# Gated linear attention and a top-1 mixture of experts in one kernel: the fullest expert's first layer is given 320 places early, at the end of the attention part's plan

## The chip, the cores and the metric

The kernel runs on one core of a Trainium2 chip. The core has a matrix engine (TensorE, PE in the rows below), a vector engine (VectorE, DVE), a scalar engine for activations (ScalarE, ACT), a general engine (GpSimd, POOL) and a queue engine (SyncE, SP), each with its own stream of instructions. SP, ACT and POOL also trigger DMA transfers. SBUF is the working memory; PE writes to the eight banks of PSUM. The metric is device time in microseconds (us); the profile comes from one further execution with the hardware profiler.

## What the reference computes

```python
# attention: 4 sequences, 8 heads, 768 steps, 48 features; a complex state per head
a = (a_re + i a_im), scaled so that |a| <= 0.999
S_t = a_t * S_(t-1) + k_t v_t^T          # a_t scales the rows of S
y_t = q_t . Re(S_t)
# the y of all heads side by side are the tokens of the second part
x = y reshaped to (3072, 384)
logits = x @ w_gate                      # 8 experts
e = argmax(logits); g = softmax(logits)[e]
out = g * (relu(x @ w1[e]) @ w2[e])      # w1: 384 x 1024, w2: 1024 x 384, each expert its own
```

## The kernel before

**Attention.** The time axis is cut into units of 128 to 384 steps (`UNITS`, ten of them) and chunks of 128 (24 in all, six for each sequence b = 0 to 3). `front(u)` turns gates, q and k of a unit into scaled operands: logarithms, exponentials and sines on ACT, scans and products on DVE and some on POOL. Its last products go to the tile `zp`, and DMAs on SP move `zp` into `hz0` or `hz1`, the operand buffers that PE reads. `chunk(b, c)` works on PE: scores (L416, masked by DVE into `am`), transposed keys (L409), the products with the state (L428) and with v (L435), the new state (L443), and a product with `turn` (L451) whose result, the tokens with their logits, ACT copies to `xg` (L454).

**Routing.** `route(b, r0, r1)` takes some chunks' tokens: DVE finds the largest logit (L467 and following, `lg` to `oh`), PE counts places (L492 to L497), DVE makes the row numbers `slot` (L504), and POOL scatters the tokens, a chunk at a time, into `xs_hbm` in device memory (L511), which has 480 places for each expert. The last sequence is routed in three pieces: chunks 0 to 2, 3 and 4, and 5. After its chunk 2, `ranks()` sorts the experts by their count so far into `order` (L533).

**Experts.** The experts go in `TURNS`, the fullest first. `weights(e)` loads w1 and w2 (1.5 MB each); `tokens(e)` loads the expert's places from `xs_hbm` into `xb` with four DMAs (for e = 0 two of them from ACT) and DVE transposes them into `xrt` (L686). `expert(e)` makes the first layer in eight groups of three matmuls, each group into a bank of its own (L701), with a relu to `ht` by ACT (L707) or DVE (L704) in turns; then the second layer in tiles of 128 places (L720), scaled by DVE (L651) and scattered by POOL (L640). An fp32 matmul is two records in the trace, so an expert's first layer is 48 records.

**What sets the order.** Each part is a `Plan`: every step names its engine, an estimated duration and the keys that it reads and writes, and `order()` searches with some randomness for a good order. The engines then run their streams as emitted, with waits for data and for buffers. Attention (P) and experts (M) are two plans. The matmuls, tiles and memory of the two parts are apart, and M is planned with `routed` 27 us after its start:

```python
        M.add("", 27.0, lambda: None, (), ("routed",))
        M.add("PE", 22.0, lambda: None, (), ("turned",))
```

Of the kernel before, what the change touches and what calls it, by code (L numbers as in the profile page):

```python
# [37 lines left out]
XR = 9  # L38
MINC = 256
# [128 lines left out]
def gateloop_then_moe(ctx, tc, gates, qk, v, wg, w1, w2, out):  # L168
# [68 lines left out]

    with ExitStack() as att:
# [4 lines left out]
        bAB, bZ = buf("AB", 2, [128, 2, G, TU]), buf("Z", 2, [128, 2, G, TU])  # L243
# [4 lines left out]
        zp, = buf("zp", 1, [128, 2, 2 * G * TU])  # L248
# [6 lines left out]
        hz = buf("hz", 2, [128, 2 * H * TU])  # L255
# [38 lines left out]
        def front(u):  # L294
# [50 lines left out]
            for g in range(G):  # L345
                P.add("DVE", 2 * T * 0.00105 + 0.19, lambda g=g: nc.vector.tensor_tensor_scan(
                    si[:, g, :], ones_t[:, sl], im[:, g, :], tend[:, b, g, c0:c0 + 1], ALU.mult, ALU.add),
                    (Bk, ("tend", b, c0)), (("si", g),))
# [107 lines left out]
        def route(b, r0, r1):  # L456
# [52 lines left out]
            for c in range(n):  # L509
# [6 lines left out]
                P.add("POOL", 1.27, f, (slot, ("xg", (g0 + c) % XR), ("empty", 0), ("empty", 1), ("empty", 2)), (("rows", b, r0 + c),), lat=2.0, wire=0.6)  # L516

        def ranks():
# [16 lines left out]
            P.add("", 14.0, lambda: None, ("order",), ("prefetch",))  # L535
# [44 lines left out]


    again = consts.tile([1, 1], I32, name="again")
    ok = consts.tile([128, 4], FP32, name="ok")
    f1 = consts.tile([128, NU], FP32, name="f1")
    nc.vector.tensor_scalar(out=f1, in0=chk, scalar1=5.0625, scalar2=None, op0=ALU.is_le)
    nc.vector.tensor_reduce(ok[:, 0:1], f1, axis=AX, op=ALU.min)
    lv = lend.rearrange("p b g c -> p (b g) c")
    f2 = consts.tile([128, B * G, C], FP32, name="f2")
    tt(f2, lv[:, :, 1:], lv[:, :, :C], ALU.subtract)
    nc.vector.tensor_scalar(out=f2, in0=f2, scalar1=-60.0, scalar2=None, op0=ALU.is_ge)  # L590
    nc.vector.tensor_reduce(ok[:, 1:2], f2.rearrange("p a c -> p (a c)"), axis=AX, op=ALU.min)
    f3 = consts.tile([128, B * G], FP32, name="f3")
    nc.vector.tensor_scalar(out=f3, in0=lv[:, :, C], scalar1=-100.0, scalar2=None, op0=ALU.is_ge)
    nc.vector.tensor_reduce(ok[:, 2:3], f3, axis=AX, op=ALU.min)
    nc.tensor.matmul(bank[7][:, 0:E], lhsT=ones_b, rhs=cumb, start=True, stop=True)
    f4 = consts.tile([128, E], FP32, name="f4")
    tt(f4, bank[7][:, 0:E], base, ALU.subtract)
    f5 = consts.tile([128, E], FP32, name="f5")
    nc.vector.tensor_scalar(out=f5, in0=f4, scalar1=float(MINC), scalar2=None, op0=ALU.is_ge)
    caps = consts.tile([128, E], FP32, name="caps")  # L600
    for x in range(E):
        nc.gpsimd.memset(caps[:, x:x + 1], float(CAPS[x]))
    tt(tmp, pick, bc(f4[:, None, :], [128, E, E]), ALU.mult)
    nc.vector.tensor_reduce(f4, tmp, axis=AX, op=ALU.add)
    tt(f4, f4, caps, ALU.is_le)
    tt(f4, f4, f5, ALU.mult)
    nc.vector.tensor_reduce(ok[:, 3:4], f4, axis=AX, op=ALU.min)
    okm = consts.tile([128, 1], FP32, name="okm")
    nc.vector.tensor_reduce(okm, ok, axis=AX, op=ALU.min)
    nc.tensor.matmul(bank[7][0:1, 64:65], lhsT=okm, rhs=one, start=True, stop=True)  # L610
    nc.vector.tensor_scalar(out=again, in0=bank[7][0:1, 64:65], scalar1=127.5, scalar2=None, op0=ALU.is_lt)


    with ExitStack() as ms:
# [17 lines left out]
        ev = xs_hbm.rearrange("(e s) w -> e s w", e=E)
        ENG = (mybir.EngineType.SP, mybir.EngineType.Activation)
        which = {}
# [20 lines left out]
        def weights(e):  # L655

            def f():
                which[e] = ds(nc.values_load(order[0:1, TURNS[e]:TURNS[e] + 1], engines=ENG[0:2 if e == 0 else 1], min_val=0, max_val=E - 1,
                                             skip_runtime_bounds_check_because="experts have numbers below E"), 1)
# [30 lines left out]
        def expert(e):  # L690
            s, n, h = e % 2, CAPS[TURNS[e]], e % NH
            if e:
                weights(e)
# [198 lines left out]
```

## Time and profile before

| | us |
|---|---|
| median of 3 runs (lowest, highest) | 545.51 (544.99, 546.72) |
| the profiled execution | 545.12 |
| its span, first to last instruction | 543.4 |
| PE busy | 455.4 (84%) |
| DVE busy | 269.5 (50%) |
| ACT busy | 201.2 (37%) |
| POOL busy | 113.7 (21%) |

The page cuts the span in 40 slices of 13.6 us and gives the busy share of each in tenths. PE is near 9 in slices 9 to 17 (attention), 3 and 4 in slices 18 and 19, and 9 or more from there on (experts). DVE is at 9 through most of slices 1 to 13 and at 1 among the experts. PE's busy time includes matmuls that run at half clock, and a matmul's end is modelled, so gaps between groups of records say more than the share.

### The profile page before, as it was taken

The page shows a single profiled execution, that of the slowest core. Times are in us where ns is not written, and L with a number is a line of the kernel's source. Part 1 is how long each engine was busy: PE and PEld are TensorE (multiplying, and loading weights), DVE is VectorE, ACT ScalarE, POOL GpSimd, SP SyncE. Part 2 cuts the span into 40 slices and gives each one's busy share as a digit, 9 for nine tenths or more (in the row PEclk, how much of TensorE's full clock was granted, in tenths as well). Part 3 has the DMA queues.
Part 4 walks back from the last instruction along what each step waited for, and adds up shares of the span by engine and source line. Part 5 has one row for each costly group of instructions (what it writes and reads, how often), then busy time and mean ns, then how long its engine had stood idle before and what let it go on. Part 6 is the DMA issues. An engine that isn't in the chain of part 4 may idle for free. (4 is left out here: it accounts for less than half of the span.)

```text
span 543.4 us, 7115 instructions
## 1 busy us (share of the span) xinstructions
PE 455.4 (84%) x2690; PEld 320.0 (59%) x2690; DVE 269.5 (50%) x432; ACT 201.2 (37%) x289; POOL 113.7 (21%) x125
## 2 busy tenths in 40 slices
PE   0046879298988989993499999999999999999995
PEld 0035769297877979992245554555555555555553
DVE  6989999999999799743121211002111111111111
ACT  6968888977787756641000100000000000000000
POOL 6263042173302450252000010210200011012102
PEclk9997669688989989997599999999999999999998
DMA  8596493969999775265992770141823370001001
GB/s 262 162 259 190 135 265 115 281 168 316 258 254 260 190 225 154 58 213 216 284 326 55 268 200 1 36 145 36 283 84 91 117 261 15 16 19 43 29 3 54
DMA packets 47226, 86.19 MB, mean 159 GB/s; under 512 B 21057, under 2 KB 36700, under 8 KB 45137
## 3 DMA queue, kind: packets, MB, share of 16 engines
q1 hardware_dynamic: 42704, 75.20, 47.9%
q0 software_dynamic: 3200, 9.86, 4.9%
q10 hardware_dynamic: 1280, 0.61, 0.5%
q8 instruction: 23, 0.38, 0.3%
q14 instruction: 19, 0.15, 0.1%
HBM read 53.93 MB, written 13.24 MB: 124 GB/s over the span
## 5 line engine op out<-in xcount | busy, mean ns | idle before, releaser
L701 PE MATMUL bank<-xrt,w1b 128*128 128x416 f32 (+3 forms) x384 | 141.1, 521 | 10.9 <-DVE xrt L686 10.9
L720 PE MATMUL bank<-w2b,ht 128*128 128x384 f32 (+1 forms) x512 | 138.7, 487 | 0.0
L701 PEld LDWEIGHTS bank<-xrt,w1b 128*128 128x128 f32 x384 | 73.8, 193 | 72.9 <-issue 39.9
L720 PEld LDWEIGHTS bank<-w2b,ht 128*128 128x128 f32 (+1 forms) x512 | 76.7, 170 | 59.0 <-issue 11.6
L707 ACT ACTIVATE ht<-bank 128x416 f32<-128x416 f32 (+3 forms) x32 | 16.5, 517 | 255.9 <-PE bank L701 255.9
L416 PE MATMUL bank<-hz 128*128 128x128 f32 x384 | 63.7, 324 | 38.8 <-DMA hz<-zp 38.4
L416 PEld LDWEIGHTS bank<-hz 128*128 128x128 f32 x384 | 58.0, 234 | 41.2 <-issue 39.1
L640 POOL DMA_INDIRECT out_dram<-yo,gi x24 | 23.6, 982 | 255.2 <-DVE yo L651 238.4
L704 DVE TENSOR_SCALAR ht<-bank 128x416 f32<-128x416 f32 (+3 forms) x32 | 18.9, 590 | 114.0 <-PE bank L701 110.3
L651 DVE TENSOR_SCALAR yo<-bank,gi 128x384 f32<-128x384 f32 x24 | 14.8, 618 | 92.7 <-PE bank L720 92.7
L181 DVE TENSOR_TENSOR zp<-Z,cs 128x1152 f32<-128x1152 f32 (+2 forms) x40 | 48.4, 1246 | 0.5 <-DMA hz<-zp 0.2
L435 PE MATMUL bank<-am,v 128*48 128x128 f32 x384 | 28.7, 290 | 11.6 <-DVE am L181 11.4
L181 DVE TENSOR_TENSOR am<-bank,causal 128x512 f32<-128x512 f32 x48 | 32.2, 681 | 11.4 <-PE bank L416 7.8
L181 POOL TENSOR_TENSOR AB<-AB,C 128x1152 f32<-128x1152 f32 (+2 forms) x9 | 20.8, 2316 | 75.7 <-ACT C L280 68.1
L511 POOL DMA_INDIRECT xs_hbm<-xg,slot x24 | 27.7, 1154 | 41.2 <-DVE slot L504 23.2
L443 PE MATMUL bank<-v,kt 128*96 128x48 f32 x320 | 33.8, 263 | 2.6 <-ACT kt L411 2.6
L443 PEld LDWEIGHTS bank<-v,kt 128*96 128x96 f32 x320 | 32.5, 181 | 3.6 <-ACT kt L411 2.7
L451 PE MATMUL bank<-turn,yt 128*128 128x104 f32 x192 | 30.5, 309 | 2.9 <-ACT yt L439 1.8
L181 POOL TENSOR_TENSOR Z<-Z,AB 128x1152 f32<-128x1152 f32 (+2 forms) x9 | 22.2, 2470 | 48.1 <-ACT AB L280 42.6
L335 DVE TENSOR_TENSOR_SCAN D<-AB,lend,C 128x384 f32<-128x384 f32 (+2 forms) x30 | 31.1, 1074 | 0.3
L578 ACT ACT_TABLE_LOAD x23 | 29.5, 1283 | 3.3 <-DVE cs L351 2.2
L451 PEld LDWEIGHTS bank<-turn,yt 128*128 128x128 f32 x192 | 27.1, 218 | 5.9 <-ACT yt L439 2.7
(122 smaller groups left out, 434.4 us busy)
## 6 DMA issues: line engine op xcount, KB each, us to landing
w1b<-in_w_dram SPq DMA_DIRECT2D x8, 1536.0 KB, 6.7
w2b<-in_w_dram SPq DMA_DIRECT2D x8, 1536.0 KB, 10.2
hz<-zp SPq DMA_DIRECT2D x24, 432.0 KB, 7.5
AB<-in_gates_dram SPq DMA_DIRECT2D x12, 576.0 KB, 4.8
Z<-in_qk_dram SPq DMA_DIRECT2D x12, 576.0 KB, 5.0
v<-in_v_dram SPq DMA_DIRECT2D x8, 576.0 KB, 8.0
hz<-zp SPq DMA_DIRECT2D x8, 288.0 KB, 4.5
hz<-zp SPq DMA_DIRECT2D x12, 192.0 KB, 7.1
```

The lines of the kernel that those rows point to most:

```text
L181: (eng or nc.vector).tensor_tensor(out=o, in0=a, in1=b, op=op)
L335: P.add("DVE", 2 * T * 0.00105 + 0.19, lambda g=g: nc.vector.tensor_tensor_scan(d[:, g, :], a[:, g, :], c[:, g, :], lend[:, b, g, c0:c0 + ...
L416: nc.tensor.matmul(SC[hf][:, (h % 4) * 128:(h % 4) * 128 + 128], lhsT=hk[:, h], rhs=hq[:, h], start=True, stop=True)
L435: nc.tensor.matmul(YT[ps, (h // 2) * 128:(h // 2) * 128 + 128], lhsT=V[:, cl, h * D:h * D + D], rhs=am[2 * par + hf][:, h % 4, :], start=( ...
L443: nc.tensor.matmul(ST[0:96, h * D:h * D + D], lhsT=kt[par][:, h * 96:h * 96 + 96], rhs=V[:, cl, h * D:h * D + D], start=(c == 0 and h == 0 ...
L451: nc.tensor.matmul(XT[:, p * 104:p * 104 + 104], lhsT=yt[par][:, p * 128:p * 128 + 128], rhs=turn[:, p, :], start=True, stop=True)
L511: i = nc.gpsimd.indirect_dma_start(out=xs_hbm[:, :], out_offset=bass.IndirectOffsetOnAxis(ap=R[slot][:, c:c + 1], axis=0), in_=xg[:, (g0 + ...
L578: nc.scalar.preload_act_table_set("natural_log_exp_and_others" if P.cur == "LE" else "trig_and_small")
L640: i = nc.gpsimd.indirect_dma_start(out=out[:, :], out_offset=bass.IndirectOffsetOnAxis(ap=index, axis=0), in_=y, in_offset=None, bounds_ch ...
L701: nc.tensor.matmul(HB[hb][:, 0:n], lhsT=w1b[e % NW][:, c:c + 128], rhs=xrt[s][:, d, 0:n], start=(d == 0), stop=(d == DT - 1))
L704: M.add("DVE", 0.6, lambda f_=f_, hb=hb: nc.vector.tensor_scalar_max(ht[h][:, f_, 0:n], HB[hb][:, 0:n], 0.0), (("H", hb),), (("ht", h, f_),))
L720: nc.tensor.matmul(OB[ob][p0:p0 + m, 0:DM], lhsT=ht[t % NH][:, f_, c0:c0 + m], rhs=w2b[t % NV][:, f_ * DM:f_ * DM + DM], start=(f_ == 0), ...
```

## The change

The first 320 places of the fullest expert (`EARLY` = 10 blocks of 32) are loaded, transposed and put through the first layer at the end of the attention plan. They hold only tokens that were routed by chunk 2 of the last sequence. The other 160 places follow in the expert plan as before, into the same `ht`. The buffers `hz`, `AB`, `Z` and `zp` of attention serve as the first two pairs of weight buffers, as `xb`, as `xrt` and as the first `ht`. The scatter of a chunk that is added to the attention plan after the early rows waits until those are loaded (the keys `xbA`). The check of the kernel's own assumptions moves into the expert plan, and `front` of the last unit is added to the plan ahead of the chunks of the unit before it.

```diff
+EARLY = 10
+    w1b, w2b = [z[:, 0:DT * F] for z in hz], [z[:, DT * F:2 * DT * F] for z in hz]
+    xb = [... for t in bAB]
+    xrt = [... for t in bZ]
+    ht = [zp...]
...
 -                P.add("POOL", 1.27, f, (slot, ..., ("empty", 2)), (("rows", b, r0 + c),), lat=2.0, wire=0.6)
+                P.add("POOL", 1.27, f, (slot, ..., ("empty", 2)) + tuple(("xbA", x) for x in range(4)), (("rows", b, r0 + c),), lat=2.0, wire=0.6)
...
+        def early_rows():
+...
+            P.add("SP", 0.5, lambda: which.update({0: expert_of(0, mybir.EngineType.SP)}), ("order",), (("which", 0),))
+            for i in range(4):
+                last = P.add("SP", 0.65, lambda i=i: nc.sync.dma_start(
+                    xb[0][32 * i:32 * i + 32, None, 0:EARLY, :], xv[:, which[0], 0:EARLY, 104 * i:104 * i + 96]),
+                    (("which", 0), "xb0") + tuple(("rows", B - 1, c) for c in range(3)), (("xbA", i),), lat=2.0, wire=0.8)
+            for z in range(2):
+                P.add("SP", 0.65, f, (("which", 0), "hz0"), (("w1", 0, z),), lat=1.9, wire=2.6)
+            P.add("SP", 0.65, lambda: nc.sync.dma_start(w2b[0][:, None, :], w2v[:, which[0], :]), ..., after=[last])
+            for j in range(0, EARLY, 4):
+                P.add("DVE", ..., lambda j=j, j1=j1: turn_rows(0, j, j1), ..., (("xrtA", j),))
+
+        def early_layer():
+            n = 32 * EARLY
+            for f_ in range(FT):
+                bk, key = ((bank[7], "ones"), (bank[3], ("KT", 1)), (bank[5], "ST"))[f_ % 3]
+                def f(f_=f_, bk=bk):
+                    for d in range(DT):
+                        c = d * F + f_ * 128
+                        nc.tensor.matmul(bk[:, 0:n], lhsT=w1b[0][:, c:c + 128], rhs=xrt[0][:, d, 0:n], start=(d == 0), stop=(d == DT - 1))
+                P.add("PE", 1.5, f, (("w1", 0, f_ // 4),) + tuple(("xrtA", j) for j in range(0, EARLY, 4)), (key,))
+                P.add("ACT", act_t(n), lambda f_=f_, bk=bk: nc.scalar.activation(ht[0][:, f_, 0:n], bk[:, 0:n], func=ACT.Relu),
+                      (key, "ht0"), (("htA", f_),))
...
-                front(u)
+                if u < NU - 1:
+                    front(u)
+                if u == NU - 2:
+                    front(NU - 1)
+                    early_rows()
...
+            early_layer()
             for i in P.order():
...
-        M.add("", 27.0, lambda: None, (), ("routed",))
-        M.add("PE", 22.0, lambda: None, (), ("turned",))
+        M.add("", 6.0, lambda: None, (), ("routed",))
...
-            s, nb = e % 2, CAPS[TURNS[e]] // 32
+            s, n0, nb = e % 2, 0 if e else EARLY, CAPS[TURNS[e]] // 32
...
-                        nc.tensor.matmul(HB[hb][:, 0:n], lhsT=w1b[e % NW][:, c:c + 128], rhs=xrt[s][:, d, 0:n], ...)
+                        nc.tensor.matmul(HB[hb][:, 0:n - n0], lhsT=w1b[e % NW][:, c:c + 128], rhs=xrt[s][:, d, n0:n], ...)
```

The order of instructions around the seam follows. PE, from the last product of attention on; before, what comes next is the count for the last chunk's route, the check and then the first expert's layer:

```order
L451 MATMUL bank6_67<-turn_97,yt1_155 128x104 x4
L492 LDWEIGHTS before_108
L492 MATMUL bank2_63<-oh_168,before_108 128x8
L494 LDWEIGHTS ones_b_111
L494 MATMUL bank2_63<-cumb_125,ones_b_111 128x8
L595 LDWEIGHTS ones_b_111
L595 MATMUL bank7_68<-cumb_125,ones_b_111 128x8
L610 MATMUL bank7_68<-one_73,okm_2033 1x1
L701 MATMUL bank0_61<-xrt0_2047,w1b0_2040 128x480 x3
L701 MATMUL bank1_62<-xrt0_2047,w1b0_2040 128x480 x3
```

In the changed kernel the same place reads as follows; the line numbers are those of the changed kernel (L473 is the product with `turn`, L514 and L516 are the count, L590 the early layer), `hz0` holds w1 and `Z0` the transposed tokens:

```order
L473 MATMUL bank6_67<-turn_97,yt1_160 128x104 x4
L590 MATMUL bank7_68<-Z0_137,hz0_139 128x320 x3
L514 LDWEIGHTS before_108
L514 MATMUL bank2_63<-oh_171,before_108 128x8
L516 LDWEIGHTS ones_b_111
L516 MATMUL bank2_63<-cumb_125,ones_b_111 128x8
L590 MATMUL bank5_66<-Z0_137,hz0_139 128x320 x3
L590 MATMUL bank7_68<-Z0_137,hz0_139 128x320 x3
L590 MATMUL bank3_64<-Z0_137,hz0_139 128x320 x3
```

One group of the early layer now stands ahead of the last chunk's count and seven behind it (the other four in banks 7, 3, 5 and 3). After these come the first two tiles of the expert's second layer, 16 matmuls of 128x384, then the eight groups of 128x160 for its other places.

ACT, from the copy of the last chunk's tokens on, before; L670 are its two triggers of loads of the first expert's rows:

```order
L454 COPY xg0_158<-bank6_67 128x416
L477 ACTIVATE ex_164<-sub_163 128x8
L658 TENSOR_LOAD order_123
L670 ISA
L670 DMA xb0_2062<-xs_hbm 32x15x96
L670 ISA
L670 DMA xb0_2062<-xs_hbm 32x15x96
L707 ACTIVATE ht0_2049<-bank0_61 128x480
```

And ACT in the changed kernel; L592 is the relu of the early layer, L736 the load of the expert's last five blocks of rows:

```order
L476 COPY xg0_163<-bank6_67 128x416
L499 ACTIVATE ex_167<-sub_166 128x8
L592 ACTIVATE zp_141<-bank7_68 128x320
L592 ACTIVATE zp_141<-bank5_66 128x320
L256 TENSOR_LOAD order_123
L736 ISA
L736 DMA AB0_135<-xs_hbm 32x5x96
L592 ACTIVATE zp_141<-bank7_68 128x320
L736 ISA
L736 DMA AB0_135<-xs_hbm 32x5x96
L592 ACTIVATE zp_141<-bank3_64 128x320
```

Two relus of the early layer stand ahead of the first trigger, one between the two triggers, and five behind.

DVE, at the route of the last chunk, in the changed kernel; L260 transposes the early rows:

```order
L489 TENSOR_REDUCE lg_128<-xg0_163 128x8
L489 TENSOR_REDUCE mx_165<-lg_128 128x1
L260 STREAM_TRANSPOSE Z0_137<-AB0_135 128x4x3x32 x2
L260 STREAM_TRANSPOSE Z0_137<-AB0_135 128x2x3x32
L182 TENSOR_TENSOR sub_166<-lg_128,mx_165 128x8
L506 SCALAR_TENSOR_TENSOR eq_169<-sub_166,rev_106 128x8
```

Before, `sub` followed `mx` at once; now the three transposes of the early rows stand between them, behind the two steps that read the last chunk's logits.

## Rows read from the trace of the kernel before

**Rows 1.** PE's waits from 262 us on: us in total, times, longest.

```profile
PE bank L701 <- DVE xrt L686: 10.9, 1, 10.9
```

**Rows 2.** Windows: us, busy by engine (records), then PE clock, DMA share, GB/s.

```profile
200.00:225.00 25.00, 25.00 (x248) 24.07 (x246) 23.66 (x57) 17.42 (x30) 3.30 (x3) 0.88 0.46 125
...
260.00:543.00 283.00, 272.09 (x896) 150.52 (x896) 47.53 (x87) 16.54 (x32) 25.53 (x26) 0.98 0.37 112
```

**Rows 3.** Timeline around the seam: start, us, work, count [idle before and its releaser].

```profile
247.30 0.98 POOL L511 DMA_INDIRECT xs_hbm<-xg,slot  x1 [0.31 <-issue]
...
247.80 1.14 PE L451 MATMUL bank<-turn,yt 128*128 128x104 f32 x8 [0.74 <-ACT yt L439]
...
249.51 0.21 DVE L467 TENSOR_REDUCE lg<-xg 128x8 f32<-128x32 f32 x1 [3.44 <-ACT xg L454]
...
252.54 0.16 DVE L504 TENSOR_REDUCE slot<-z 128x1 int32<-128x8 f32 x1 [1.03 <-DMA xs_hbm<-xg,slot]
...
253.58 0.99 POOL L511 DMA_INDIRECT xs_hbm<-xg,slot  x1 [5.09 <-DVE tmp L181]
...
257.44 2.23 SPq L670 DMA_DIRECT2D xb<-xs_hbm  x4
257.51 1.20 ACTq L670 DMA_DIRECT2D xb<-xs_hbm  x2
...
263.72 0.35 SPq L662 DMA_DIRECT2D w1b<-in_w_dram  x1
263.78 1.85 DVE L686 STREAM_TRANSPOSE xrt<-xb 128x384 f32<-128x384 f32 x4 [8.78 <-DMA xb<-xs_hbm]
...
265.70 19.75 PE L701 MATMUL bank<-xrt,w1b 128*128 128x480 f32 x42 [10.87 <-DVE xrt L686]
```

**Rows 4.** Timeline of the step that makes the early rows possible, columns as in Rows 3.

```profile
239.07 0.22 DVE L533 TENSOR_REDUCE order<-tmp 128x8 int32<-128x64 f32 x1
239.19 0.98 POOL L511 DMA_INDIRECT xs_hbm<-xg,slot  x1 [0.30 <-issue]
...
240.33 0.38 SPq L662 DMA_DIRECT2D w1b<-in_w_dram  x1
```

**Rows 5.** The tile xb from 230 to 300 us: landing of its loads.

```profile
DMA to landing us min/median/max: 3.0/4.8/15.5
```

**Rows 6.** Timeline: weight loads and matmuls at full clock, columns as in Rows 3.

```profile
271.60 0.19 PEld L701 LDWEIGHTS bank<-xrt,w1b 128*128 128x128 f32 x1 [0.21 <-issue]
...
272.00 0.19 PEld L701 LDWEIGHTS bank<-xrt,w1b 128*128 128x128 f32 x1 [0.21 <-issue]
...
285.29 2.74 PE L720 MATMUL bank<-w2b,ht 128*128 128x384 f32 x8
```

**Rows 7.** Timeline of earlier PE work: two waits, and a group of scores.

```profile
129.36 0.65 PE L435 MATMUL bank<-am,v 128*48 128x128 f32 x8 [2.07 <-DVE am L181]
...
154.71 0.98 PE L435 MATMUL bank<-am,v 128*48 128x128 f32 x8 [1.92 <-DVE am L181]
...
241.73 1.08 PE L416 MATMUL bank<-hz 128*128 128x128 f32 x8
```

**Rows 8.** Windows of 1 us after waits of PE, columns as in Rows 2.

```profile
131.00:132.00 1.00, 1.00 (x9) 1.00 (x8) 1.00 (x2) 1.00 (x2) 0.00 (x0) 0.50 1.00 336
137.00:138.00 1.00, 1.00 (x7) 0.95 (x5) 0.58 (x1) 1.00 (x2) 0.00 (x0) 0.59 1.04 283
154.00:155.00 1.00, 0.29 (x4) 0.29 (x6) 1.00 (x3) 1.00 (x2) 0.00 (x0) 0.94 0.87 171
158.00:159.00 1.00, 0.55 (x8) 0.25 (x4) 1.00 (x1) 0.59 (x2) 0.00 (x0) 0.86 1.08 221
...
270.00:271.00 1.00, 1.00 (x3) 0.53 (x2) 0.00 (x0) 0.04 (x1) 0.00 (x0) 0.54 1.13 479
```

**Rows 9.** Groups by shape, ACT from 250 us on: busy us, mean ns, idle before.

```profile
L707 ACT ACTIVATE ht<-bank 128x384 f32<-128x384 f32 x12 | 5.9, 490 | 93.1 <-PE bank L701 93.1
```

More of the change, by code (lines that the diff above doesn't have):

```diff
@@ L236, in gateloop_then_moe, with expert_of, turn_rows @@
     nc.gpsimd.memset(empty.bitcast(I32)[:, W - 1:W], 1 << 20)
+    keep = ctx.enter_context(tc.tile_pool(name="keep", bufs=1))
+    bAB, bZ, hz = ([keep.tile(shp, FP32, name=f"{nm}{i}") for i in range(2)] for nm, shp in (
+        ("AB", [128, 2, G, TU]), ("Z", [128, 2, G, TU]), ("hz", [128, 2 * H * TU])))
+    zp = keep.tile([128, 2, 2 * G * TU], FP32, name="zp")
+    w1b, w2b = [z[:, 0:DT * F] for z in hz], [z[:, DT * F:2 * DT * F] for z in hz]
+    xb = [t.rearrange("p a g t -> p (a g t)")[:, 0:CAP * 3].rearrange("p (n c) -> p n c", c=96) for t in bAB]
+    xrt = [t.rearrange("p a g t -> p (a g t)")[:, 0:CAP * DT].rearrange("p (d c) -> p d c", d=DT) for t in bZ]
+    ht = [zp.rearrange("p a t -> p (a t)")[:, 0:FT * CAP].rearrange("p (f c) -> p f c", f=FT)]
+    w1v, w2v = (w.rearrange("(e p) f -> p e f", p=128) for w in (w1, w2))
+    xv = xs_hbm.rearrange("(e j p) w -> p e j w", e=E, p=32)
+    sv = xs_hbm.rearrange("(e s) w -> s e w", e=E)
+    ev = xs_hbm.rearrange("(e s) w -> e s w", e=E)
+    which = {}
+    def expert_of(e, eng):
+        return ds(nc.values_load(order[0:1, TURNS[e]:TURNS[e] + 1], engines=(eng,), min_val=0, max_val=E - 1,
+                                 skip_runtime_bounds_check_because="experts have numbers below E"), 1)
+    def turn_rows(s, b0, b1):
+        nc.vector.transpose(xrt[s][:, :, 32 * b0:32 * b1].rearrange("p d (b t) -> p b d t", t=32),
+                            xb[s][:, b0:b1].rearrange("p b (d c) -> p b d c", d=DT))
     with ExitStack() as att:
@@ L515, in f @@
                     tc.add_to_no_dep_group("rows", i.ins)
-                P.add("POOL", 1.27, f, (slot, ("xg", (g0 + c) % XR), ("empty", 0), ("empty", 1), ("empty", 2)), (("rows", b, r0 + c),), lat=2.0, wire=0.6)
+                P.add("POOL", 1.27, f, (slot, ("xg", (g0 + c) % XR), ("empty", 0), ("empty", 1), ("empty", 2)) + tuple(("xbA", x) for x in range(4)), (("rows", b, r0 + c),), lat=2.0, wire=0.6)
         def ranks():
@@ new lines, in early_layer @@
+        def early_layer():
[9 more added lines that the diff above has]
+                      (key, "ht0"), (("htA", f_),))
+            P.add("seam", 7.0, lambda: None, tuple(("rows", B - 1, c) for c in range(C)), ("seam",))
@@ L591, in gateloop_then_moe @@
[L591 to L608, printed above, removed]
@@ L655, in weights @@
         def weights(e):
-            def f():
-                which[e] = ds(nc.values_load(order[0:1, TURNS[e]:TURNS[e] + 1], engines=ENG[0:2 if e == 0 else 1], min_val=0, max_val=E - 1,
-                                             skip_runtime_bounds_check_because="experts have numbers below E"), 1)
-            M.add("SP", 0.3, f, (), (("which", e),), after=rows[-1:])
+            M.add("SP", 0.5, lambda: which.update({e: expert_of(e, mybir.EngineType.SP)}), (), (("which", e),), after=rows[-1:])
             for wb, wv, nb, nm in ((w1b, w1v, NW, "w1"), (w2b, w2v, NV, "w2")):
@@ L728, in gateloop_then_moe @@
         with tc.manual_schedule():
-            weights(0)
             for e in range(E):
                 expert(e)
+                if e == 0:
+                    check(M)
                 if e < E - 1:
@@ L735, in gateloop_then_moe @@
                     M.add("PE", 0.5, lambda: flag.append(nc.values_load(again[0:1, 0:1], min_val=0, max_val=1, skip_runtime_bounds_check_because="0 or 1")),
[L736 removed]
+                          (("H", 0), "again"), ())
             for i in M.order():
```

110 lines of the change are left out of this document (69 added, 41 removed).

## The prediction

> **What bounds the kernel now.** I read the slices of the page first, then the waits of PE, then the seam between attention and experts instruction by instruction, and last the order of both kernels there. From 262 us on PE has one single wait, for the transposed tokens of the first expert [rows 1], and in 260 to 543 us it is busy for 272.09 of 283 us at a clock of 0.98 [rows 2]. So the expert part is bound by PE alone: what PE starts earlier at the seam comes off the end one for one, as long as no later wait takes its place. At the seam PE ends the last product of attention at 247.80 + 1.14 = 248.94 us, which I call E, and starts the first expert's layer at 265.70 [rows 3]. Between stand 16.76 us in which PE has three tiny counts to do.
>
> What fills them is a chain without slack: the logits of the last chunk reach DVE at 249.51; the row numbers at 252.54 wait 1.03 us until the scatter of chunk 4, started at 247.30, has landed (5.2 us); the last scatter starts at 253.58 and has landed at 257.44 (3.9 us), when SP and ACT trigger the loads of the rows; the transposes start at 263.78 and PE at 265.70 [rows 3]. The pause has a second price: PE comes back at half clock. The first 42 records took 19.75 us [rows 3], while at full clock one starts every 0.40 us [rows 6], 16.8 us in all; the difference is 2.9 us, and the clock rose in the slice of 270 us [rows 8].
>
> **The change part by part.** All is reckoned from E. At full clock the work of PE from the first expert matmul to the end is 543.40 - 265.70 - 2.9 = 274.8 us.
>
> *The early layer itself.* 48 records of 320 columns, at 0.40 us for 480 columns [rows 6] 0.267 us each, are 12.8 us. The 48 records of 160 columns are 6.4 us by their columns; a group of eight records with 128 columns takes 1.08 us, 0.135 each [rows 7], and a weight load 0.19 [rows 6], so 6.4 to 9.1 us; I take 0.145 each, 7.0, near the 128-column row. Together 19.8 in place of 19.2. With 0.2 for the counts of the check, which used to lie in the pause, 274.8 - 19.2 + 7.0 + 0.2 = 262.8 us are left behind the early layer.
>
> *When it can start.* The ranks were known at 239.29, w1 was triggered at 240.33, and the third scatter of the last sequence started at 239.19 [rows 4]. With 3.9 to 5.2 us to land, four triggers of some 0.6 us (four took 2.23 [rows 3]) and 3.0 to 4.8 us for the loads [rows 5], the early rows would be there between 248.3 and 251.4. In the new order PE has some 2.5 us more of attention's work left behind the count for the ranks than before, so I take L, their landing, as E. On DVE the transposes now stand behind the first two steps of the last chunk's route, which end about E + 1.0. Four transposes of 15 blocks took 1.85 us [rows 3]; three of 10 blocks take 1.3 to 1.5. PE starts at **E + 2.5**. A gap of that size brings half clock: after waits of 2.07 and 1.92 us [rows 7] the clock went down within two us and stayed down from about 131.0 to 137.8 and from 154.9 to 158.3 [rows 8], which costs 1.7 to 3.4 us of PE work.
>
> *Where it stops.* Each group is 1.6 us and needs a free bank. Four groups run without a further relu than the first two. The fifth goes to bank 7 again and needs the third relu, and on ACT a trigger for the last rows stands ahead of that relu. That trigger waits for the last scatter. SP shows that a waiting trigger holds what is behind it: the second expert's w1, which waits for no rows, was triggered only at 263.72, behind the row loads [rows 3]. I take ACT to do the same; the other end is that it holds nothing. The trigger is set free so: the scatter of chunk 3 now waits for L, that of chunk 4 starts 1.3 later and lands 5.2 later, at E + 6.8; slot and scatter as before 1.04 later, landing 3.9 later, **E + 11.7** (before: E + 8.5). Then 0.6 for the trigger (two took 1.20 [rows 3]), 0.45 for a relu of 320 (0.49 for 384 [rows 9]) and 0.2 for two hand-overs: the fifth group starts at E + 12.9. The first four, 6.4 us and 3.4 for the clock from E + 2.5 on, with the count of 0.2 between, end by E + 12.5, so the clock's price is hidden under the hold. Four groups more: the early layer ends at **E + 19.3**.
>
> The Trainium skill says the same of ACT: TensorE: Matmul & The Clock Gate, Part 1, on the engines' queues, has the scalar engine work strictly first in, first out. By that rule the hold is sure and the time is the forecast; were it not so, the time would be that of the first rival. No run here yet shows ACT behind a waiting trigger.
>
> *What I cost at nothing.* The last five blocks of rows: triggered by E + 13.2, landed 4.8 later [rows 5], transposed by E + 19; PE has 32 records of the second layer first, at 2.74 us for eight [rows 6] 11 us, so they are needed at E + 30 and have 11 us of cover. The second expert's w1 goes behind the row loads as before, at about 265 against 263.72, and is needed at E + 39: cover of more than 10 us. The check's steps on DVE lie beside experts' matmuls, where DVE is busy for 47.53 of 283 us [rows 2]. If a cover fails, its excess falls on PE in full.
>
> *Attention.* The instructions up to the seam are the same, but the order is searched anew. In 200 to 225 us DVE is busy for 23.66 of 25 us and PE all the time, at a clock of 0.88 [rows 2]: a new order has little idle time to win on DVE; it can dodge that dip (12% of 25, 3.0 us) or meet one more like that of 131 us (3.4 us). I take 0, with -4 to +4.
>
> *Sum.* With E = 248.94 the span ends at 248.94 + 19.3 + 262.8 = 531.0, 12.4 us under 543.4. The profiled execution took 545.12, 0.4 below the median of the runs, so 532.7 to 533.1: **533 us**.
>
> **Rivals.** *Nothing holds ACT*, or the last scatter lands by the time the relu is due. Then the layer runs through, E + 2.5 + 12.8 + 0.2 and 0 to 3.4 for the clock, E + 15.5 to E + 18.9: 529 to 532, in the middle 530. For it speaks only that no row shows ACT held. Chance 0.18.
>
> *Attention becomes longer.* Two more dips of the clock like that at 131 us, or as much in waits of DVE for ACT in the new order: 4 to 8 us later, 537 to 541. Against it: the same instructions on engines as full as before. Chance 0.16.
>
> *PE stays at half clock through the early layer*, since it works in bursts. 48 records of 0.533 us are 25.6, the end E + 28.3: 542. Against it: both dips [rows 8] ended while PE was busy, within seven us. Chance 0.08.
>
> *Slower: the early rows land late.* They queue behind the 1.5 MB of w1. DVE holds the last chunk's route behind their transposes, and POOL the scatters of chunks 3 to 5, so every us that L is later moves the last scatter, ACT and PE by one. The gain of 12.4 is gone at L = E + 12.4. Triggered up to about E - 4, with the longest landing seen, 15.5 us [rows 5], L is E + 11.5 and the time 544; it would take two to three us more to be slower. The median of 4.8 speaks against it. Chance 0.06, of which 0.04 slower.
>
> **How the numbers follow.** The forecast has the remaining 0.52; with attention moved by up to three us it spans 530 to 536. Down to 527 the range takes in the first rival with attention somewhat shorter, up to 540 the most of the second: 0.52 + 0.18 + 0.12, a little over 0.8. A measurement of this kernel tells about 0.3%, 1.6 us, from no change. Faster by more: the forecast, the first three rivals and none of the last, 0.94; the same 0.02; slower 0.04.
>
> **What would show it.** In the changed profile: L590 starts 2 to 3 us after the last L473; its first four groups partly at half clock, the fifth behind a wait of PE for ACT that ends 1 to 1.5 us after ACT's trigger of L736, 11 to 13 us after the last L473; L736 some three us later, counted from the last L473, than L670 was; from the fifth group to the end no wait of PE. Wrong it would be if the last L473 lies more than four us from 248.94, if L260 waits for its rows beyond E + 3, if the wait for ACT is missing, or if PE waits among the experts for weights that SP now triggers behind something else.

## The result, and the profile after

The changed kernel takes 530.28 us (median of 4, 528.97 to 531.65), the kernel before 545.25 (4 runs, 541.07 to 546.72): a ratio of 0.9738, 95% interval 0.9678 to 0.9797. The forecast was 533 with a range of 527 to 540. The profiled execution took 530.8 us with a span of 529.0, so that the spans differ by 14.4 us. The ratio and its interval are taken over all runs; the quotient of the two medians is 0.9725, and in the runs below the two differ by up to 0.004.

PE's waits from 225 us to the end are all that is left of the pause (us in total, times, longest):

```profile
PE bank L590 <- issue: 3.3, 1, 3.3
PE bank L590 <- ACT zp L592: 0.8, 1, 0.8
PE bank L473 <- ACT yt L461: 0.7, 1, 0.7
```

The timeline of the seam after the change (start, us, work, count, idle before and its releaser), which answers to [rows 3, 4]:

```profile
234.04 1.89 SPq L573 DMA_DIRECT2D hz<-in_w_dram  x2
235.24 0.98 POOL L533 DMA_INDIRECT xs_hbm<-xg,slot  x1 [0.30 <-issue]
...
243.03 1.95 SPq L567 DMA_DIRECT2D AB<-xs_hbm  x4
...
244.71 1.14 PE L473 MATMUL bank<-turn,yt 128*128 128x104 f32 x8 [0.74 <-ACT yt L461]
247.77 1.30 DVE L260 STREAM_TRANSPOSE Z<-AB 128x384 f32<-128x384 f32 x3 [0.95 <-DMA AB<-xs_hbm]
248.45 0.98 POOL L533 DMA_INDIRECT xs_hbm<-xg,slot  x1 [12.03 <-DMA AB<-xs_hbm]
249.17 3.54 PE L590 MATMUL bank<-Z,hz 128*128 128x320 f32 x6 [3.33 <-issue]
...
249.73 0.98 POOL L533 DMA_INDIRECT xs_hbm<-xg,slot  x1 [0.30 <-issue]
...
252.60 5.50 PE L590 MATMUL bank<-Z,hz 128*128 128x320 f32 x18
...
253.56 0.16 DVE L526 TENSOR_REDUCE slot<-z 128x1 int32<-128x8 f32 x1 [0.53 <-DMA xs_hbm<-xg,slot]
254.53 0.99 POOL L533 DMA_INDIRECT xs_hbm<-xg,slot  x1 [3.62 <-DVE slot L526]
...
257.69 0.64 ACTq L736 DMA_DIRECT2D AB<-xs_hbm  x1
257.72 3.29 SPq L736 DMA_DIRECT2D AB<-xs_hbm  x6
258.38 0.44 ACT L592 ACTIVATE zp<-bank 128x320 f32<-128x320 f32 x1 [3.04 <-PE bank L590]
...
258.87 6.73 PE L590 MATMUL bank<-Z,hz 128*128 128x320 f32 x24 [0.77 <-ACT zp L592]
...
261.29 0.74 DVE L260 STREAM_TRANSPOSE Z<-AB 128x384 f32<-128x384 f32 x2 [7.56 <-DMA AB<-xs_hbm]
...
265.44 10.48 PE L786 MATMUL bank<-hz,zp 128*128 128x384 f32 x32
...
275.76 6.68 PE L767 MATMUL bank<-Z,hz 128*128 128x160 f32 x48
```

E, the end of the attention's last product, is 244.71 + 1.14 = 245.85, against 248.94 before [rows 3]. The early layer starts 3.3 us behind it. Its first group takes 3.54 us for six records; the next three run until 258.10; the fifth waits 0.77 us for the third relu, which came only behind ACT's trigger at 257.69. The second layer starts at 265.44, E + 19.6, and the last five blocks are transposed 13 us before L767 reads them. So 14.4 us are made of two parts: attention ended 3.1 us earlier, and from E to the end it is 529.0 - 245.85 = 283.15 us instead of 543.4 - 248.94 = 294.46, that is 11.3 less.

The 3.3 us in which PE stands still ahead of the early layer are called the gap below. The windows of PE's clock (busy time by engine as in [rows 2], then clock, DMA share, GB/s) show its second price:

```profile
200.00:225.00 25.00, 22.03 (x243) 20.24 (x239) 23.27 (x54) 15.43 (x27) 5.13 (x5) 1.00 0.37 103
...
247.00:253.00 6.00, 3.83 (x9) 2.50 (x10) 2.67 (x14) 0.46 (x2) 2.16 (x3) 0.50 0.76 305
...
255.00:529.00 274.00, 267.04 (x935) 153.12 (x933) 46.13 (x94) 18.33 (x39) 25.94 (x27) 1.00 0.37 116
```

From 247 to 253 us the granted clock is 0.50, the 1.2 GHz level; from 255 on it is full. In 200 to 225 us it is now 1.00 where it was 0.88 [rows 2].

### The profile page after: what moved, and what is told of

It reads as the page before. It is cut to its first block, busy times and chain, and to the rows that moved or that the text cites. A ratio compares the mean times of both kernels' runs of the same rounds, so it can differ in the third digit from the quotient of the medians.

```text
span 529.0 us, 7236 instructions
## 1 busy us (share of the span) xinstructions
PE 450.7 (85%) x2738; PEld 319.0 (60%) x2738; DVE 266.4 (50%) x433; ACT 206.0 (39%) x299; POOL 115.1 (22%) x125
## 5 line engine op out<-in xcount | busy, mean ns | idle before, releaser
L767 PE MATMUL bank<-Z,hz 128*128 128x416 f32 (+2 forms) x288 | 90.9, 468 | 0.0
L707 POOL DMA_INDIRECT out_dram<-yo,gi x24 | 23.5, 977 | 243.2 <-DVE yo L718 229.5
L767 PEld LDWEIGHTS bank<-Z,hz 128*128 128x128 f32 x288 | 52.1, 190 | 35.4 <-issue 20.3
L773 ACT ACTIVATE ht<-bank 128x416 f32<-128x416 f32 (+2 forms) x20 | 10.1, 511 | 154.8 <-PE bank L767 154.8
L786 PE MATMUL bank<-hz,ht 128*128 128x384 f32 (+1 forms) x176 | 59.5, 487 | 0.0
L786 PEld LDWEIGHTS bank<-hz,ht 128*128 128x128 f32 (+1 forms) x176 | 30.5, 175 | 19.9 <-issue 2.4
L770 DVE TENSOR_SCALAR ht<-bank 128x416 f32<-128x416 f32 (+2 forms) x20 | 11.6, 582 | 58.9 <-PE bank L767 58.9
L786 PE MATMUL bank<-w2b,ht 128*128 128x384 f32 (+1 forms) x128 | 37.5, 487 | 0.0
L786 PE MATMUL bank<-w2b,zp 128*128 128x384 f32 (+1 forms) x112 | 37.5, 486 | 0.0
L767 PE MATMUL bank<-Z,w1b 128*128 128x448 f32 (+1 forms) x96 | 36.1, 517 | 0.0
L431 PE MATMUL bank<-ident,hz 96*128 96x96 f32 x160 | 22.4, 275 | 16.0 <-DMA hz<-zp 14.4
```

The costliest lines, as they stand in the source:

```text
L431: nc.tensor.transpose(KT[hf][:, (h % 4) * 96:(h % 4) * 96 + 96], hk[0:96, h], ident[0:96, 0:96])
L707: i = nc.gpsimd.indirect_dma_start(out=out[:, :], out_offset=bass.IndirectOffsetOnAxis(ap=index, axis=0), in_=y, in_offset=None, bounds_ch ...
L767: nc.tensor.matmul(HB[hb][:, 0:n - n0], lhsT=w1b[e % NW][:, c:c + 128], rhs=xrt[s][:, d, n0:n], start=(d == 0), stop=(d == DT - 1))
L770: M.add("DVE", 0.6, lambda f_=f_, hb=hb: nc.vector.tensor_scalar_max(ht[h][:, f_, n0:n], HB[hb][:, 0:n - n0], 0.0), (("H", hb),), (("ht", ...
L773: M.add("ACT", 0.6, lambda f_=f_, hb=hb: nc.scalar.activation(ht[h][:, f_, n0:n], HB[hb][:, 0:n - n0], func=ACT.Relu), (("H", hb),), (("ht ...
L786: nc.tensor.matmul(OB[ob][p0:p0 + m, 0:DM], lhsT=ht[t % NH][:, f_, c0:c0 + m], rhs=w2b[t % NV][:, f_ * DM:f_ * DM + DM], start=(f_ == 0), ...
```

## The experiments

The runs were made in four groups, each on a chip of its own: a0 to k3, where the kernel before took 552.24 us; a1 to k5, 545.86; k6, k7 and kw, 551.30; k8, 552.32. The ratios of the changed kernel agree between chips, the times do not, so runs are compared by their ratio to the kernel before. Of each profile the same places are read as above, in us, counted from its own E (the end of the attention's last product):

| run | E | early layer starts | last rows triggered | second layer starts | from there to the end | ratio, 95% interval |
|---|---|---|---|---|---|---|
| changed kernel | 245.85 | +3.3 | +11.8 | +19.6 | 263.6 | 0.9738, 0.9678 to 0.9797 |
| a0_after | 252.23 | +2.4 | +11.5 | +19.0 | 263.7 | 0.9740, 0.9698 to 0.9781 |
| a1_after | 243.21 | +4.0 | +13.9 | +21.4 | 263.7 | 0.9723, 0.9667 to 0.9780 |
| k1_sp | 251.78 | +3.4 | +12.0 | +18.8 | 262.3 | 0.9684, 0.9639 to 0.9729 |
| k1_again | 248.05 | +3.3 | +11.6 | +18.5 | 262.3 | 0.9680, 0.9628 to 0.9732 |
| k2_late | 249.62 | +2.6 | +13.3 | +22.5 | 263.5 | 0.9784, 0.9749 to 0.9818 |
| k4_warm | 243.31 | +4.3 | +11.7 | +19.3 | 265.0 | 0.9791, 0.9732 to 0.9851 |
| k5_sp_warm | 244.43 | +4.3 | +14.0 | +17.4 | 262.4 | 0.9691, 0.9636 to 0.9746 |
| k6_early_sp | 253.15 | +2.5 | +13.8 | +18.3 | 262.1 | 0.9668, 0.9633 to 0.9702 |
| k7_early_act | 252.84 | +1.5 | +12.5 | +18.4 | 263.4 | 0.9723, 0.9680 to 0.9766 |
| k8_rows_first | 253.31 | +2.1 | +12.9 | +18.2 | 262.4 | 0.9667, 0.9620 to 0.9714 |

The column E falls into two sets, and most of the difference lies in one place. In the changed kernel's first profile ACT's copy to `yt` and PE's product behind it ran like this near 226 us:

```profile
225.66 0.58 ACT L461 COPY yt<-bank 128x512 f32<-128x512 f32 x1 [2.69 <-PE bank L457]
...
227.19 1.10 PE L473 MATMUL bank<-turn,yt 128*128 128x104 f32 x8
```

and in a0_after, on another chip, like this:

```profile
230.11 0.69 DVE L182 TENSOR_TENSOR am<-bank,causal 128x512 f32<-128x512 f32 x1 [5.70 <-remote]
230.16 0.58 ACT L461 COPY yt<-bank 128x512 f32<-128x512 f32 x1 [7.02 <-remote]
...
230.80 2.04 PE L473 MATMUL bank<-turn,yt 128*128 128x104 f32 x8 [3.28 <-ACT yt L461]
```

DVE and ACT stand still and the profile names no engine of this core that released them ("remote"); PE then waits 3.3 us and comes back at half clock (0.53 in 230 to 236 us). From the first of the six scatters that start near 222 us to E it is 23.3 us in the profiles of the new order without this stall and 28.1 to 29.6 in those with it. All eight profiles on the chips of a0, k6 and k8 have it, kw_before among them, with a wait of PE of 3.2 to 4.1 us; the six on the other two chips, the kernel before among them, do not. What causes it is open.

### The changed kernel again (a0_after, a1_after)

> The changed kernel once more, as the baseline of the runs beside it. Expected 530.3 us, 0.972 to 0.975 of the time before; the fifth group of the early layer again behind a wait of PE for ACT of about 0.8 us. If the gain of 14 to 15 us was partly a matter of one chip, it would come out nearer to the forecast of 533.

> The changed kernel again, as the baseline of the three runs beside it: 0.974 of the time before, the early layer from 2.4 to 3.4 us behind the attention's last product, the fifth group behind ACT 12.4 to 13.0 us behind it, the second layer 19.0 to 19.6 us behind it.

537.12 us on the one chip, 529.12 on the other; the ratios 0.9740 and 0.9723 repeat the first. The wait for ACT was 1.71 and 1.24 us, not 0.8. In a1_after the early rows reached DVE at E + 2.6, the latest of all, and everything behind them, ACT's trigger included, came two us later than expected: the second layer at E + 21.4.

### All last loads from SP (k1_sp, k1_again)

```diff
-            if e == 0:
-                M.add("ACT", 0.5, lambda: which.update({"ACT": expert_of(0, mybir.EngineType.Activation)}), (), (("which", "ACT"),))
...
-                eng, dma, wh = ("ACT", nc.scalar, "ACT") if e == 0 and i % 2 else ("SP", nc.sync, e)
+                eng, dma, wh = "SP", nc.sync, e
```

> All four loads of the last rows are triggered by SP, none by ACT, so that nothing stands ahead of the third relu on ACT. Theory (ACT's waiting trigger holds the relus, and with them the fifth group): the wait of PE for ACT of 0.77 us goes, the fifth group follows the fourth at once, third relu about 2 us earlier, the early layer and the kernel end 0.8 us earlier, 529.5. Rival (the trigger holds nothing; the fifth group waits for its bank or for something else that is late): the wait stays, 530.3. A second rival: the 1.2 us by which the row loads are now later on SP reach PE, which then waits before the second part of the first layer: 531 or more.

> All four loads of the last rows from SP, again, as the baseline of the run that adds dummy products to it: 0.7% (3.8 us) under the changed kernel if the first measurement holds, of which the seam can explain at most 0.8 to 1.7 us (the hold) and the new plan of the experts 1.35 us; if only the hold counts, 0.2 to 0.3%.

The timeline of k1_sp:

```profile
255.21 3.54 PE L590 MATMUL bank<-Z,hz 128*128 128x320 f32 x6 [3.44 <-issue]
...
258.64 12.12 PE L590 MATMUL bank<-Z,hz 128*128 128x320 f32 x42
...
263.81 4.30 SPq L734 DMA_DIRECT2D AB<-xs_hbm  x8
```

The wait is gone: 42 records run in one piece, and no relu waits for the trigger at 263.81. So ACT's trigger is what held the fifth group; the attention's order is otherwise the same. The Trainium skill, TensorE: Matmul & The Clock Gate, Part 1, has ScalarE's queue strictly first in, first out; the trace agrees, with waits of 0.77, 1.71 and 1.24 us with the triggers and none without.

The gain, 0.56% and 0.43% (3.1 and 2.3 us) over the changed kernel in the same group, is more than the hold. In the profiles the seam gives 1.3 us (18.8 and 18.5 against 19.6, 19.0 and 21.4) and the part behind it 1.35 us (262.3 against 263.6 to 263.7), because the planner found another order for the experts with the same steps: 0.67 us less until PE's last product ends, and 5.6 us instead of 6.2 to 6.3 behind it.

### The first weights behind the early rows (k2_late)

```diff
-            for i in P.order():
+            seq = P.order()
+            w1s = [i for i in seq if P.ops[i]["name"].startswith("('w1'")]
+            seq = [i for i in seq if i not in w1s]
+            at = max(seq.index(i) for i in seq if P.ops[i]["name"].startswith("('xbA'")) + 1
+            seq[at:at] = w1s
+            for i in seq:
```

> The same order, but SP triggers the first expert's first weights behind the four loads of the early rows instead of ahead of them. Theory (the scatter of chunk 2, which the early rows wait for, landed late, 7.8 us after its start, because it queued behind those 1.5 MB): it lands in 4 to 5 us, the early rows are triggered about 240 instead of 243, landed before the end of the attention's last product, and the early layer starts 0.8 to 1.5 us earlier, 2 to 2.5 us behind that product; since ACT's trigger holds the fifth group, the end comes only 0 to 0.8 us earlier. Rival (the scatter is slow of itself): the triggers stay near 243 and the early layer starts as before. Second rival: the weights are now what is late; the early layer starts behind them at 250 to 252, up to 2 us later, and the time is 530 to 532.

```profile
239.03 0.98 POOL L533 DMA_INDIRECT xs_hbm<-xg,slot  x1 [0.30 <-issue]
...
242.59 3.01 SPq L567 DMA_DIRECT2D AB<-xs_hbm  x4
...
245.85 1.49 SPq L573 DMA_DIRECT2D hz<-in_w_dram  x2
...
250.22 0.98 POOL L533 DMA_INDIRECT xs_hbm<-xg,slot  x1 [0.30 <-issue]
...
258.92 0.16 DVE L526 TENSOR_REDUCE slot<-z 128x1 int32<-128x8 f32 x1 [2.88 <-DMA xs_hbm<-xg,slot]
...
263.84 8.42 PE L590 MATMUL bank<-Z,hz 128*128 128x320 f32 x24 [2.34 <-ACT zp L592]
```

The scatter of chunk 2 now lands within 3.6 us (239.03 to 242.59), where it took 7.8 in the changed kernel (235.24 to 243.03) and 6.1 in a0_after on the same chip: the traffic of the weights was what delayed it. The Trainium skill, DMA: Bandwidth & Descriptors, Queues, rings and completion order, has each DMA engine take turns between its queues packet by packet; that a scatter next to 1.5 MB takes 6.1 to 8.3 us instead of 3.6 agrees with it in direction. But the delay is only moved. The scatter of chunk 4, from 250.22 to 258.92, now takes 8.7 us beside the weights instead of the 3.8 to 5.1 of the changed kernel's three profiles, ACT's trigger is free later, PE waits 2.3 us for it, and the second layer starts at E + 22.5. That is 2.4 us slower than the changed kernel beside it by ratio (the intervals overlap): no part of the expected gain, and more than either rival.

### Attention's new order alone (k3_noearly)

```diff
+                if o["name"].startswith(("('xbA'", "('xrtA'", "('htA'")) or i in layer:
+                    continue
...
-            s, n0, nb = e % 2, 0 if e else EARLY, CAPS[TURNS[e]] // 32
+            s, n0, nb = e % 2, 0, CAPS[TURNS[e]] // 32
```

> The attention's new order is kept, but the early loads, transposes, products and relus are left out, and the first expert's first layer is done whole behind the pause, as it was before the change. Theory (the new order by itself ends the attention 3.1 us earlier, because it dodges the dip of TensorE's clock ahead of its end; the other 11.3 us come from the early layer): last product of attention at 244.5 to 245.5, pause of 16 to 17 us, 542 us, 0.994 of the time before. Rival (the 3.1 us come from the early work's company, or are chance): the last product at 248 to 249 and 545 us, and the early layer alone is worth 14 to 15.

549.56 us against 552.24, 0.9933 (0.9899 to 0.9967): attention's order alone is worth 0.67%, 3.7 us (1.8 to 5.6); the medians alone give 2.7. From this to a0_after the ratio falls by 0.0193, so the early layer is worth 10.7 us, by an estimate from the two intervals to within some 3 us. The theory's 3.1 and 11.3 are inside both. In the timeline the pause is back:

```profile
253.32 1.14 PE L473 MATMUL bank<-turn,yt 128*128 128x104 f32 x8 [0.74 <-ACT yt L461]
...
270.57 14.98 PE L772 MATMUL bank<-Z,hz 128*128 128x480 f32 x30 [14.08 <-issue]
```

From E (254.46) to the end it is 549.6 - 254.46 = 295.1 us, as before the change (294.5). E itself, expected at 244.5 to 245.5 from the one profile, was 254.46, some 5 us of it the stall described above. Even on one chip the same order of attention ended between 243.2 and 248.1 us (a1 to k5) or between 249.6 and 254.5 (a0 to k3), so one pair of profiles cannot size this part. Only the timed runs carry it.

### PE kept busy through the gap (k4_warm, k5_sp_warm)

```diff
+WARM = 20
...
+            def g():
+                f()
+                for _ in range(WARM if gc == NT - 1 else 0):
+                    nc.tensor.matmul(SC[0][:, 0:128], lhsT=ident, rhs=causal, start=True, stop=True)
+            P.add("PE", 0.95, g, (("yt", par),), ("XT",))
```

> The changed kernel with 20 dummy products of 128 columns on PE right behind the attention's last product (2.7 us of extra work into a bank that nothing reads), so that PE is busy in the gap ahead of the early layer. Theory (the half clock of the early layer's first two groups is a price of the gap, 3.4 us of PE work, but hidden under ACT's hold of the fifth group): the first group takes 1.6 us instead of 3.4, the fourth group ends 2 to 3 us earlier, PE then waits 3 to 5 us for ACT, the fifth group starts 12.4 to 13.0 us behind the last product as before, and the time is that of the changed kernel within 1 us. Rival (the time of the early layer is set by PE and its clock, the hold is chance): 2 to 3 us faster. Second rival (the gap has nothing to do with the clock): first group at half clock all the same, same time.

> Both: all four loads of the last rows from SP, and the 20 dummy products behind the attention's last product. Theory: with the hold gone the price of the half clock is no longer hidden, so that now the dummy products pay: the early layer runs through in 13.4 us from 2.7 to 3.5 us behind the last product, the second layer starts 16.3 to 17.2 us behind it (18.8 with the loads from SP alone), 1.6 to 2.7 us faster than with the loads from SP alone. Rival (clock does not matter): the same time as with the loads from SP alone.

The timeline of k4_warm:

```profile
243.15 4.65 PE L479 MATMUL bank<-causal,ident 128*128 128x128 f32 x40
...
247.63 1.78 PE L595 MATMUL bank<-Z,hz 128*128 128x320 f32 x6
...
249.30 5.09 PE L595 MATMUL bank<-Z,hz 128*128 128x320 f32 x18
...
256.01 6.73 PE L595 MATMUL bank<-Z,hz 128*128 128x320 f32 x24 [1.61 <-ACT zp L597]
```

The clock is at 1.00 from 240 to 257 us and the first group takes 1.78 us instead of 3.54: the half clock is the price of the gap. With ACT's triggers in place the fifth group still starts 12.7 us behind E: that price was hidden under the hold. But 20 products are 40 records and took 4.65 us, not 2.7, so that the early layer started some 0.5 us later than its rows allowed, and PE's wait for ACT was 1.6 us, not 3 to 5. The time was not within 1 us: by ratio it is 0.68% of the time before, 3.7 us, above the changed kernel's in the same group (the intervals overlap). The profile, taken of the fastest of the six runs, does not show why: its second layer starts at E + 19.3, and the 1.3 us more behind that all lie behind the last product of the experts. This stays open.

Without the triggers (k5_sp_warm) the second layer starts at E + 17.4, 1.1 to 1.4 us earlier than without dummies, about what the overlong dummies left of the expected 1.6 to 2.7. In the timed runs, 0.9691 against 0.9680, nothing of it is left to see; the range of E alone is wider than that.

### Rows first (k6_early_sp, k7_early_act, k8_rows_first)

```diff
+            behind(named("('w1'")[1:], named("('xbA'")[-1])
+            behind(named("('xrtA'"), named("('lg'")[-1], 0)
+            behind(named("RT")[-1:], [i for i in seq if i in layer][1])
```

`behind` moves instructions of the emitted order behind another one (with 0, ahead of it). k6 is on top of k1_sp, k7 on top of the changed kernel; k8 is k6 with `[1:]` left out.

> Four moves in the emitted order, on top of the loads of the last rows from SP alone: the second half of the first expert's first weights goes behind the early rows' loads on SP; the three transposes of the early rows go ahead of the last chunk's first two route steps on DVE; the last chunk's count on PE goes behind the second early group instead of the first. Theory (the gap of 2.4 to 4.0 us ahead of the early layer is the rows' landing behind the weights' traffic plus DVE's order, and it brings the half clock): the rows are triggered 4.5 to 6 us ahead of the end of the attention's last product instead of 1 to 5, the early layer starts 0.2 to 1.2 us behind that product, at full or nearly full clock, and the second layer starts 13.5 to 15.5 us behind it, against 18.5 to 18.8 with the loads from SP alone: 3 to 5 us faster than that, 0.959 to 0.963 of the time before. Rival (something else holds the start, the weights above all, whose second half now lands late): start or a later group waits 2 us or more, second layer at 17 to 19, 0.966 to 0.969.

> The same moves in the emitted order, but with two of the last rows' loads on ACT, as in the changed kernel. Theory (ACT's waiting trigger holds the fifth group whatever comes ahead of it): the early layer starts as early as in the run beside it, four groups end by 7 to 8 us behind the last product, and PE then waits 2 to 4 us for ACT; the trigger is set free 9 to 11 us behind the last product, since the scatters of chunks 3 and 4 wait less for the early rows; second layer 17 to 19 us behind it; 0.967 to 0.971 of the time before, 3 to 4 us slower than the run beside it. Rival (the hold no longer binds, since the last scatter is also earlier): within 1.5 us of the run beside it.

> As the earlier run with all loads of the last rows on SP and the four moves, but the whole of the first expert's first weights goes behind the early rows' loads on SP, not only its second half. Theory (it is the weights' traffic, even half of it, that makes the scatter of chunk 2 land 6 to 8 us after its start, and with it the early rows late): the scatter lands in 3.5 to 4.5 us, the rows are triggered 5 to 7 us ahead of the end of the attention's last product and are there before it, the early layer starts 0.2 to 1.5 us behind that product at full or soon full clock, and the second layer starts 14 to 17 us behind it (18.3 with half of the weights ahead): 0.960 to 0.965 of the time before. Rival (the weights are now what is late): the start or the second group waits for them to 2.5 us or more behind the product, PE goes to half clock, second layer at 18 to 20, 0.967 to 0.971.

The timelines of k6_early_sp and of k8_rows_first:

```profile
242.56 0.98 POOL L533 DMA_INDIRECT xs_hbm<-xg,slot  x1 [0.30 <-issue]
...
249.17 1.96 SPq L567 DMA_DIRECT2D AB<-xs_hbm  x4
...
254.21 1.30 DVE L260 STREAM_TRANSPOSE Z<-AB 128x384 f32<-128x384 f32 x3 [2.52 <-DMA AB<-xs_hbm]
...
255.61 6.17 PE L592 MATMUL bank<-Z,hz 128*128 128x320 f32 x12 [2.46 <-issue]
```

```profile
242.72 0.97 POOL L533 DMA_INDIRECT xs_hbm<-xg,slot  x1 [0.30 <-issue]
...
246.27 2.97 SPq L567 DMA_DIRECT2D AB<-xs_hbm  x4
...
249.49 1.49 SPq L573 DMA_DIRECT2D hz<-in_w_dram  x2
251.78 1.30 DVE L260 STREAM_TRANSPOSE Z<-AB 128x384 f32<-128x384 f32 x3
...
255.43 6.43 PE L592 MATMUL bank<-Z,hz 128*128 128x320 f32 x12 [2.12 <-DVE sm L501]
```

In k6 half of the weights ahead of the scatter is enough to make it land after 6.6 us; the rows come at E + 1.1 and PE starts at E + 2.5, not at E + 0.2 to 1.2: the theory failed, its rival held. In k8 the scatter lands after 3.6 us and the rows are transposed by E; still PE starts at E + 2.1. The releaser printed there, a step of DVE, writes nothing that PE reads, and the only other input are the weights, triggered from 249.49 on (a half of them landed 6.5 us after its trigger in the changed kernel). So PE waits for the weights, by exclusion, since no row shows their landing in k8: the theory failed here too, and the rival held, with a start 0.4 us earlier than it said. Rows and weights share the DMA engines in these last us of attention; whichever goes first, PE has a gap of 1.5 to 2.5 us and the half clock behind it, and the second layer starts at E + 18.2 to 18.4 in all three. 0.9668 and 0.9667 are the lowest ratios of the study, but not told apart from k1_sp's 0.968. k7 shows the hold again (a wait of 1.84 us for ACT, the trigger at E + 12.5 and not at 9 to 11), yet its second layer starts as early as k6's, since its gap was 1 us shorter in this profile. It is 0.55% slower than k6; the profiles show 1.4 us of these 3 in the experts' order, and no more.

### Dummy products in the old pause (kw_before)

```diff
+            for _ in range(44):
+                nc.tensor.matmul(SC[0][:, 0:128], lhsT=ident, rhs=causal, start=True, stop=True)
```

> The kernel before the change with 44 dummy products of 128 columns on PE in the pause between attention and experts, behind the last chunk's count (into a bank that nothing reads; some 10 us of work at full clock, more at half). Theory (the 2.9 us by which the first 42 records after the pause were longer than at full clock are a price of the idle pause): the records of 480 columns start at 0.40 us from the first one on, and the time is 2 to 3 us, 0.4 to 0.6%, under the kernel before. Rival (they are slow for another reason, such as the loads that run beside them): still 2.9 us long, same time. If the dummy products overrun the pause, by as much slower; the gap in front of the first expert product shows that.

1.0051 (1.0019 to 1.0083), half a per cent slower. The windows show that it did not do what it was made for, and something else:

```profile
256.00:262.00 6.00, 5.35 (x27) 5.35 (x27) 1.43 (x12) 0.21 (x1) 0.99 (x1) 0.50 0.09 36
263.00:269.00 6.00, 6.00 (x56) 6.00 (x55) 0.00 (x0) 0.00 (x0) 0.00 (x0) 1.00 1.26 199
270.00:273.00 3.00, 0.19 (x2) 0.09 (x2) 2.52 (x11) 0.00 (x0) 0.00 (x0) 1.00 0.98 396
273.00:280.00 7.00, 6.36 (x8) 2.86 (x9) 0.59 (x2) 0.57 (x1) 0.00 (x0) 0.51 1.06 372
```

The 88 records of the dummies ran until 269.65, nearly to the end of the old pause. They stood ahead of the check's two counts on PE, DVE's steps of the check waited for these, and the transposes of the rows stood behind those steps: a new gap from 270 to 273 us, and the expert's products at half clock all the same, starting at E + 18.8 instead of E + 16.8 [rows 3]. The 2.9 us of the old pause are thus not measured by taking them away. But the rival falls: PE was at 0.50 with the DMA engines at 0.09 and at 1.00 with them at 1.26, so the loads beside it are not what sets the clock. One thing more bears on the attention: its order here is the old one, yet the clock in 200 to 225 us was 1.00, not the 0.88 of [rows 2].

## Why the prediction was right, and where it was off

**The mechanism** held. PE alone bounds the rest: from the fifth group to the end there is no wait. ACT's trigger was freed at E + 11.8 (forecast 11.7), the fifth group started at E + 13.0 (12.9), the second layer at E + 19.6 (19.3), and k1_sp showed the trigger to be the cause, against the first rival. The half clock came in the gap and was hidden under the hold, as k4_warm shows. The late rows of the last rival came, by 1.9 us here and 2.6 in a1_after, not by twelve. The last rows, the second expert's w1 and the check, costed at nothing, cost nothing: PE waits for none of them.

That the trigger came within 0.1 us of its forecast is luck, though. The chain that frees it was forecast as L at E, 0.3 and 1.3 to the start of the scatter of chunk 4 (the 0.3 is in the sum without a reason), 5.2 for its landing, 1.04, and 3.9 for the last landing. It measured 1.9, 0.7 and 1.3, then 3.8, 1.0 and 3.2: two us too late, then two us too short. In a1_after, where the rows came at E + 2.6 and the scatter of chunk 4 took 5.0, the trigger came at E + 13.9 and the second layer at E + 21.4.

**The sum** was right by two errors that offset each other in part:

- *Attention, taken as 0.* It gave 3.1 us in the profiles and 3.7 (1.8 to 5.6) in k3_noearly. The step named what could happen, a dodge of the dip in 200 to 225 us, and the clock there did rise from 0.88 to 1.00; the size was near the edge of the allowed -4 to +4. That this dodge is the cause is not shown: in kw_before the clock there was 1.00 under the old order.
- *From E on, taken as 12.4 less.* It is 11.3 in the profiles and 10.7 in the runs. The shortfall of 1.1: the second layer 0.3 late, and 263.6 instead of 262.8 us behind it. The 160-column records were not at fault (48 in 6.68 us, forecast 7.0). Of the 0.8 us, 0.6 lie behind PE's last product: the last output step on DVE starts at 522.85, 6.2 us ahead of the span's end, where it was 5.6 before.
- *L, taken as E.* The rows came at E + 1.9, up to E + 2.6 in a1_after. The step that failed is the scatter's landing of 3.9 to 5.2 us. The 3.9 was read where the DMA engines were nearly idle (0.13 in 253 to 257 us), the 5.2 near the end of the weights' traffic, 6.4 us behind their last trigger (0.99 in 247 to 251 us). Started 0.6 to 1.2 us behind the first trigger of 1.5 MB of weights it took 6.1 to 8.3 in seven profiles. So PE started 0.8 us later than the E + 2.5 of the forecast. That delay of PE disappeared under the hold; the delay of the rows moves the hold itself, and was made good only by the shorter landings above.

```profile
522.85 0.62 DVE L718 TENSOR_SCALAR yo<-bank,gi 128x384 f32<-128x384 f32 x1 [1.96 <-PE bank L786]
523.74 0.98 POOL L707 DMA_INDIRECT out_dram<-yo,gi  x1 [0.32 <-POOLq L808]
```

These are the last steps of the changed kernel's timeline, ahead of the end at 529.0.

## What to carry to other kernels

When work is moved into a pause, take a transfer's landing time from a place with the same traffic beside it: the loads that the move itself brings forward slow the very transfer that it waits for, and here putting them behind it only moved the delay. Look at every in-order engine that the moved work now shares with a waiting trigger, and let an engine that nothing waits for issue it. And when a planner searches its order anew, expect a few us of either sign from the parts that were not touched; leave the moved work out under the new order to measure them.

## What was not expected of the hardware

- With the same order of instructions the attention ended at 243.2 to 248.1 us on one chip and 249.6 to 254.5 on another. All profiles of the second have a stall of ACT, DVE and PE near 228 us whose releaser the profile does not name, with PE at half clock behind it, together some 5 to 6 us; those of the first have none. The rest of the spread is not explained.
- A scatter of 128 rows landed in 3.6 us without weights triggered ahead of it, in 6.3 to 6.6 us with 0.75 MB (k6, k7) and in 6.1 to 8.3 us with 1.5 MB: half the bytes hardly helped.
- In k2_late the 2.3 us wait inside the early layer was followed by a slower fifth group (24 records in 8.42 us instead of 6.73, at a clock of 0.52 and 0.63 in 264 to 268 us), so a hold can cost more than its own length. Behind the waits of 1.24 to 1.84 us at the same place in a1_after, k4_warm, a0_after and k7_early_act the records ran at full speed.
